# Moving rounding steps and masks, a fourth buffer for keys and values, and a last chunk in token order, in a kernel of retention and a feed-forward block

## Chip, cores, metric

One core of a Trainium2 chip. Time is device microseconds (us) of one execution; all runs quoted are of the fast state, except half_pe, of which there is one run whose state is unknown. GB/s is what the core's 16 DMA engines moved; a DMA share of 1.0 means that their packets took, summed, as long as 16 engines have. PE is TensorE, DVE VectorE, ACT ScalarE, POOL GpSimd, SP SyncE; SPq and ACTq are the DMA-issuing queues. "In the chain" means in the profile's chain of work that ended last, which gives a start and a length without overlap.

## The reference

```python
q, k, v: (8, 8, 576, 64)                 # batch, heads, tokens, width
scores = q @ k.T / 8
ret = scores * gamma_h ** (i - j) for i >= j, else 0
attn = ret @ v
x = attn.transpose(0, 2, 1, 3).reshape(4608, 512)
h = x @ w_in                             # 512 x 2048
g = h * erf(softplus(h))
out = g @ w_out                          # 2048 x 512; w_in and w_out arrive as float64
```

## The kernel before

Tokens are handled in 36 pieces of 128 and 9 chunks of 4 pieces; a piece is attended with a running state, so it needs queries and keys transposed, and keys and values in rows. From piece 8 on the transposed ones are loaded as squares (`load_squares`) that DVE transposes. The feed-forward block is cut in four quarters of `w_in` and `w_out`; the first quarter (`g == 0`) of each chunk runs interleaved with attention, the rest (from about 350 us on) alone. Both products use a seven-product scheme for 2 x 2 blocks. The weights arrive as 64-bit words and are rounded to float32 in steps, spread over the blocks. In the profile's lines qT and kT are transposed queries and keys, s on PE the scores, sT the masked scores, o on PE the outputs of attention; a, e and g are the PSUM accumulators of the feed-forward products, wraw the words, wa and wb the rounded weights. All products of two tensors on DVE go through one helper, L99.

```python
def load(i, names="qkv"):                                   # all issued by SP, in program order
    ...
        elif name == "q":
            t["qs"] = load_squares(i, "q", q)               # 4 DMAs each, 2 buffers, rows of 896 bytes
            t["ks"] = load_squares(i, "k", k)
        elif name == "v" or len(pieces[i]) == 1:
            t[name] = load_rows(i, name, src, 3)            # 2 DMAs, 3 buffers, rows of 256 bytes

def transposes(i): ...;  load(i + 2, "q")                   # DVE, then the next squares
def scores(i): ...                                          # PE s, then the masks sT on DVE (L99)
def outputs(i): ...;     load(i + 3, "kv")                  # PE o, then x scaled on DVE

def rounding():                                             # a generator: each next() is one step
    while True:
        ...
        nc.scalar.activation(a_f, high_f, AF.Abs)           # L246: ACT waits here for the words
        yield
        nc.vector.tensor_scalar(...)                        # L251, then L255, L259, L264
        ...
        load_weights()                                      # next words, on SP
        if sums: yield from sums(...)

# the block that loads words, n = 1 and 2:
            if n in (1, 2):
                load_weights()
                load_weights()
            run(b.middle(), (1, 1))                         # one rounding step after each product
            firsts[n - 1].sums()
            run(seconds[n - 1].first(), (1, 1))
            run(b.last())
```

Of the kernel before, what the change touches and what calls it, by code (L numbers as in the profile page):

```python
# [15 lines left out]
ALU = mybir.AluOpType  # L16
PSUM = bass.MemoryType.PSUM

P = 128
B, H, S, D = 8, 8, 576, 64  # L20
D_MODEL, D_FF = 512, 2048
NP = H // 2
# [32 lines left out]
def kernel(  # L55
# [15 lines left out]
    n_ch = n_tok // TCH  # L71
# [26 lines left out]
    def tt(out, in0, in1, op):  # L98
        nc.vector.tensor_tensor(out=out, in0=in0, in1=in1, op=op)  # L99

    def flat(ap):
        return ap.rearrange("p h d -> p (h d)")
# [17 lines left out]
    SQ = 32  # L120
# [14 lines left out]
    def load_rows(i, name, src, bufs):  # L135
        if name == "q":
            t = raw.tile([P, NP, P * D // SQ], FP32, tag="qs", name="raw_q", bufs=bufs)
            t = t.rearrange("p a x -> p (a x)")[:, : H * D].rearrange("p (h d) -> p h d", h=H)
        else:
            t = raw.tile([P, H, D], FP32, tag=name, name=f"raw_{name}", bufs=bufs)  # L140
        for b, s0, n, r0 in pieces[i]:
            for e in range(2):
                heads = src[b, e * NP : (e + 1) * NP, s0 : s0 + n, :]
                nc.sync.dma_start(out=t[r0 : r0 + n, e::2, :], in_=heads.rearrange("h p d -> p h d"))
        return t

    def load(i, names="qkv"):
        if i < len(pieces):
            t = loaded.setdefault(i, {})
            for name in names:  # L150
                src = {"q": q, "k": k, "v": v}[name]
                if name == "q" and i < SQUARES:
                    t["q"] = load_rows(i, "q", q, 2)
                elif name == "q":
                    t["qs"] = load_squares(i, "q", q)
                    t["ks"] = load_squares(i, "k", k)
                elif name == "v" or len(pieces[i]) == 1:
                    t[name] = load_rows(i, name, src, 3)

    load(0)  # L160
    cst = cpool.tile([P, CONST_COLS], FP32, name="cst")
# [4 lines left out]
    gk, gq, gp, tri, gk2, gq2, tri2 = (cst[:, a:b] for a, b in zip(ends, ends[1:]))  # L166
    gq, gq2 = (g.rearrange("p (a i) -> p a i", a=NP) for g in (gq, gq2))
# [108 lines left out]
    def round_weights(n=1):  # L276
        for _ in range(n):
            next(round_step, None)
# [7 lines left out]
    x = {}  # L286
# [55 lines left out]
    def outputs(i):  # L342
        segments = pieces[i]
        t = live.pop(i)
        seen = [(kept[b], r0, n) for b, s0, n, r0 in segments if s0 > 0]



        b, s0, n, _ = segments[0]
        o = [ps_at.tile([P, NP, P], FP32, tag="at", name=f"o{j}") for j in range(2)]  # L350
        for p in range(NP):
            for e in range(2):
                nc.tensor.matmul(  # L353
                    o[p % 2][heads[(e + p) % 2], p // 2, :],
                    lhsT=t["v"][:, 2 * p + e, :],
                    rhs=t["sT"][:, e, p, :],
                    start=(p < 2),
                    stop=(not seen and p >= NP - 2),
                    skip_group_check=True,
                )  # L360
        for state, r0, m in seen:
            for p in range(NP):
                for e in range(2):
                    nc.tensor.matmul(  # L364
                        o[p % 2][heads[(e + p) % 2], p // 2, r0 : r0 + m],
                        lhsT=state[heads[e], p, :],
                        rhs=t["qT"][heads[e], p, r0 : r0 + m],
                        start=False,
                        stop=(p >= NP - 2),
                        skip_group_check=True,  # L370
                    )
        if n == P:
            kv = flat(o[0])[:, 2 * P :].rearrange("p (a d) -> p a d", a=NP)
            for p in range(NP):
                for e in range(2):
                    nc.tensor.matmul(  # L376
                        kv[heads[e], p, :],
                        lhsT=t["k"][:, 2 * p + e, :],
                        rhs=t["v"][:, 2 * p + e, :],
                        start=False,  # L380
                        stop=(p == NP - 1),
                        skip_group_check=True,
                    )
        c, at = i // PC, i % PC * P
        if (0, c) not in x:
            x[0, c] = x_tile()

        def scaled(j):
            by = (gq if n == P else gq2)[:, j::2, :].unsqueeze(2).to_broadcast([P, 2, P // n, n])
            dst, got = (  # L390
                y.rearrange("p a (m i) -> p a m i", i=n) for y in (x[0, c][:, j:NP:2, at : at + P], o[j][:, :2])
            )
            tt(dst, got, by, ALU.mult)

        scaled(1)
        if n == P:
            sums = kv
            if s0 > 0:
                sums = att.tile([P, NP, D], FP32, tag="sums", name="sums")
                tt(sums, kv, kept[b], ALU.add)  # L400

            if b % 2 == 0 and s0 + P + D == S:
                new = att.tile([P, NP, D], FP32, tag="last", name="last", bufs=1)
            else:
                new = att.tile([P, NP, D], FP32, tag="state", name="state")
            (nc.gpsimd if s0 > 0 else nc.vector).tensor_tensor(out=new, in0=sums, in1=gp, op=ALU.mult)
            kept[b] = new
        scaled(0)
        load(i + 3, "kv")
        if i + 1 >= SQUARES:  # L410
            weigh_values(i + 1)
# [148 lines left out]
    class Second:  # L560
# [91 lines left out]
        def store(self, half, os=slice(0, D_MODEL), queue=nc.sync, tps=(0, 1)):  # L652
            if self.g < n_g - 1:
                nc.sync.dma_start(out=od[self.c][:, half, :, os], in_=self.o[:, half, :, os])
            else:
                for tp in tps:
                    for b, s0, n, r0 in pieces[self.c * PC + 2 * half + tp]:
                        rows = out[b * S + s0 : b * S + s0 + n, os].rearrange("(r a) o -> a r o", r=SQ)
                        for a in range(n // SQ):
                            at = slice(r0 + a * SQ, r0 + (a + 1) * SQ)  # L660
                            queue.dma_start(out=rows[a], in_=self.o[at, half, tp, os])
# [3 lines left out]
    firsts = [First(g, c) for g, c in order]  # L665
    seconds = [Second(f) for f in firsts]
# [15 lines left out]
    def run(steps, rounds=(), stages=1):  # L682

        for step, _ in enumerate(steps):
            attend(min(done[0] + stages, most[0]))
            round_weights(rounds[step] if step < len(rounds) else 0)
# [25 lines left out]
    most[0] = before_chunk(3)  # L712
    attend(after_chunk(1) + 1)
    operands_x(0, 1)
    round_weights(4)
    for _ in firsts[1].first():
        attend(done[0] + 1)
        round_weights(2)
    firsts[0].erf()
    firsts[0].multiply()  # L720
    seconds[0].begin()
    for b, nxt in zip(blocks[1:], blocks[2:] + [None]):
        n = order.index((b.g, b.c))
        if isinstance(b, First):
            most_g[0] = order[n - 1][0] + 1
            if n in (1, 2):
                load_weights()
                load_weights()
            run(b.middle(), (1, 1))
            firsts[n - 1].sums()  # L730
            run(seconds[n - 1].first(), (1, 1))
            run(b.last())
            most[0] = before_chunk(n + 3)
        elif n + 2 < n_s:
            f = firsts[n + 1]
            for step, _ in enumerate(b.middle()):
                attend(min(done[0] + 1, most[0]))
                if step == 0:
                    f.erf()
                elif step == 1 and n + 2 >= n_ch:  # L740
                    operands_x(*order[n + 2])
            if n + 2 < n_ch:
                attend(after_chunk(n + 2))
                operands_x(*order[n + 2])
            run(nxt.first(), (1,))
            f.multiply()
            seconds[n + 1].begin()
            if n_ch <= n + 3 < n_s:
                load_x(*order[n + 3])
            run(b.last(), (0, 1))  # L750
        elif n + 1 < n_s:
            firsts[n + 1].erf()
            seconds[n + 1].begin()
            rest = b.rest()
            for _ in range(3):
                next(rest)
            firsts[n + 1].multiply()
            run(rest)
            firsts[n + 1].sums((0,))
            first = nxt.first()  # L760
            next(first)
            firsts[n + 1].sums((1,))
            run(first)
        else:
            run(b.rest())
# [30 lines left out]
```

## Time and profile before

| | before |
|---|---|
| median of 3 runs | 1044.54 us (1043.72 to 1046.25) |
| profiled span, granted clock | 1041.5 us, 0.994 |
| PE busy | 1019.4 us, 98% |
| longest wait of PE | 5.8 us, at 87 to 93 us |
| end of span after the last sum | 6.7 us |

The prediction below shows the lines and how they are read. Another view is engines' busy time by stretch (us:us, length, then busy us and instructions of PE, PEld, DVE, ACT, POOL, then granted clock, DMA share, GB/s). Before:

```profile
60.00:100.00 40.00, 31.24 (x255) 24.55 (x255) 32.12 (x54) 13.36 (x17) 12.06 (x11) 0.87 0.98 226
100.00:150.00 50.00, 50.00 (x501) 40.63 (x498) 37.89 (x63) 18.27 (x23) 14.34 (x15) 1.00 0.85 207
150.00:200.00 50.00, 50.00 (x494) 40.49 (x494) 38.95 (x68) 14.81 (x21) 9.52 (x10) 1.00 1.02 223
```

### The profile page before, as it was taken

What the parts mean: (1) busy time and instruction counts of PE and PEld (TensorE: products, weight loads), DVE (VectorE), ACT (ScalarE), POOL (GpSimd) and SP (SyncE); (2) the same over time, 40 slices, a digit from 0 to 9 for tenths busy, and PEclk for the clock granted to TensorE, in tenths of its full rate; (3) what the DMA queues carried; (4) which work ended last, traced back from release to release, by engine and by line L of the source; (5) the groups of instructions that cost most, each with busy time, mean ns of one, the idle gap of its engine ahead of it and who ended that gap; (6) DMA issues with size and microseconds to landing.
All of it is one profiled execution on the core that took longest, in us unless ns stands there. A gap on an engine that the chain in (4) does not pass through costs nothing.

```text
span 1041.5 us, 15938 instructions
## 1 busy us (share of the span) xinstructions
PE 1019.4 (98%) x6322; PEld 875.6 (84%) x6322; DVE 674.9 (65%) x1061; ACT 387.6 (37%) x477; POOL 123.6 (12%) x122
## 2 busy tenths in 40 slices
PE   8987999999999999999999999999999999999997
PEld 7776888888888888888888888888888888888886
DVE  3996878768866645667656656666667555555554
ACT  2352242332342444433434334444443333333431
POOL 2160222221312000100001001100100000000000
PEclk9998999999999999999999999999999999999999
DMA  9989979999994531633264523363333334444433
GB/s 193 215 218 216 237 166 247 222 204 231 215 210 139 188 123 40 243 142 143 69 253 145 179 81 142 146 237 123 121 122 121 124 129 132 130 132 124 145 96 82
DMA packets 149051, 167.28 MB, mean 161 GB/s; under 512 B 97904, under 2 KB 123632, under 8 KB 140912
## 3 DMA queue, kind: packets, MB, share of 16 engines
q1 hardware_dynamic: 147824, 165.47, 55.9%
q8 instruction: 50, 0.82, 0.4%
q10 hardware_dynamic: 1152, 0.79, 0.3%
q14 instruction: 25, 0.20, 0.1%
HBM read 119.02 MB, written 47.19 MB: 160 GB/s over the span
## 4 chain that ended last, share of the span: by engine, by line
PE 87%; DVE 5%; DMA 5%; SPq 1%; issue 1%; ACT 1%; DVEq 0%; ACTq 0%
PE a L576 23%; PE a L469 22%; PE g L576 12%; PE g L469 11%; PE e L576 6%; PE e L469 6%; PE s L335 3%; PE o L353 2%; DMA wraw<-in_moe_w_in_dram 1%; PE o L376 1%; PE o L364 1%; DMA raw_qs<-in_q_dram 1%; DVE x L99 1%; DMA raw_ks<-in_k_dram 1%; DVE t L99 1%
## 5 line engine op out<-in xcount | busy, mean ns | idle before, releaser
L469 PE MATMUL a<-x,wa 128*128 128x256 f32 x1120 | 267.3, 382 | 0.0
L469 PEld LDWEIGHTS a<-x,wa 128*128 128x128 f32 x1120 | 212.4, 191 | 29.9 <-issue 0.2
L576 PE MATMUL a<-wb,s 128*128 128x256 f32 x864 | 205.7, 381 | 0.0
L576 PEld LDWEIGHTS a<-wb,s 128*128 128x128 f32 x864 | 162.9, 190 | 23.6 <-ACT o L590 0.7
L99 DVE TENSOR_TENSOR t<-g,t 128x512 f32<-128x512 f32 x70 | 48.3, 690 | 156.0 <-ACT t L499 116.0
L469 PE MATMUL g<-x,wa 128*128 128x256 f32 x560 | 133.8, 382 | 0.2 <-DVE o L99 0.2
L469 PEld LDWEIGHTS g<-x,wa 128*128 128x128 f32 x560 | 106.1, 191 | 15.6 <-DVE o L99 0.6
L99 DVE TENSOR_TENSOR o<-a,o 128x512 f32<-128x512 f32 x108 | 74.2, 687 | 50.5 <-PE a L576 50.5
L494 ACT COPY t<-a 128x512 f32<-128x512 f32 x35 | 20.5, 586 | 187.5 <-PE a L469 187.5
L99 DVE TENSOR_TENSOR t<-t,s 128x1024 f32<-128x1024 f32 x72 | 87.4, 1254 | 0.0
L538 ACT ACTIVATE s<-t 128x1024 f32<-128x1024 f32 x72 | 72.1, 1049 | 31.2 <-DVE t L99 31.2
L266 POOL TENSOR_TENSOR wraw<-wraw 128x512 f32<-128x512 f32 x28 | 29.1, 1040 | 455.2 <-DVE wraw L264 243.4
L99 DVE TENSOR_TENSOR x<-x 128x512 f32<-128x512 f32 x116 | 77.9, 704 | 1.2
L505 ACT COPY t<-a 128x512 f32<-128x512 f32 x35 | 20.5, 586 | 152.6 <-PE a L469 152.6
L542 ACT ACTIVATE s<-s 128x1024 f32<-128x1024 f32 x72 | 72.1, 1049 | 0.4
L576 PE MATMUL g<-wb,s 128*128 128x256 f32 x288 | 68.6, 381 | 0.1
L576 PE MATMUL e<-wb,t 128*128 128x256 f32 x288 | 68.6, 381 | 0.0
L576 PE MATMUL a<-wb,t 128*128 128x256 f32 x288 | 68.5, 380 | 0.0
L576 PE MATMUL g<-wb,t 128*128 128x256 f32 x288 | 68.2, 380 | 0.0
L99 DVE TENSOR_TENSOR o<-g,o 128x512 f32<-128x512 f32 x72 | 49.3, 685 | 27.5 <-ACT o L590 22.7
L469 PE MATMUL e<-x,wa 128*128 128x256 f32 x280 | 66.8, 381 | 0.0
L99 DVE TENSOR_TENSOR sT<-s,cst 128x512 f32<-128x512 f32 x72 | 46.2, 682 | 25.9 <-PE s L335 25.9
(75 smaller groups left out, 1201.3 us busy)
## 6 DMA issues: line engine op xcount, KB each, us to landing
od<-o SPq DMA_DIRECT2D x54, 512.0 KB, 3.3
x<-xd SPq DMA_DIRECT2D x27, 1024.0 KB, 5.0
o<-od SPq DMA_DIRECT2D x27, 1024.0 KB, 4.8
raw_qs<-in_q_dram SPq DMA_DIRECT2D x96, 112.0 KB, 4.6
raw_ks<-in_k_dram SPq DMA_DIRECT2D x96, 112.0 KB, 4.3
xd<-x SPq DMA_DIRECT2D x9, 1024.0 KB, 5.1
raw_k<-in_k_dram SPq DMA_DIRECT2D x64, 128.0 KB, 4.4
raw_v<-in_v_dram SPq DMA_DIRECT2D x64, 128.0 KB, 4.4
```

What stands on the lines that cost most here:

```text
L99: nc.vector.tensor_tensor(out=out, in0=in0, in1=in1, op=op)
L266: engine.tensor_tensor(out=r_f, in0=high_f, in1=r_f, op=ALU.mult)
L335: nc.tensor.matmul(ps[e][:, p, :], lhsT=t["kT"][heads[e], p, :], rhs=t["qT"][heads[e], p, :], start=True, stop=True)
L353: nc.tensor.matmul(o[p % 2][heads[(e + p) % 2], p // 2, :], lhsT=t["v"][:, 2 * p + e, :], rhs=t["sT"][:, e, p, :], start=(p < 2), stop=(no ...
L364: nc.tensor.matmul(o[p % 2][heads[(e + p) % 2], p // 2, r0 : r0 + m], lhsT=state[heads[e], p, :], rhs=t["qT"][heads[e], p, r0 : r0 + m], s ...
L376: nc.tensor.matmul(kv[heads[e], p, :], lhsT=t["k"][:, 2 * p + e, :], rhs=t["v"][:, 2 * p + e, :], start=False, stop=(p == NP - 1), skip_gr ...
L469: nc.tensor.matmul(acc[:, j * TH : (j + 1) * TH], lhsT=weights["wa", self.g][:, a, d, j * P : (j + 1) * P], rhs=x[self.g, self.c][a][:, d, :],
L494: nc.scalar.copy(out=self.t1[:, 1], in_=self.a)
L505: nc.scalar.copy(out=self.t2[:, 0], in_=self.a)
L538: nc.scalar.activation(self.s[:, j], t, AF.Softplus)
L542: nc.scalar.activation(self.s[:, j], self.s[:, j], AF.Erf)
L576: nc.tensor.matmul(acc[:, tp, :], lhsT=left[:, j * TH + tp * P : j * TH + (tp + 1) * P], rhs=weights["wb", self.g][:, b, j, :], start=(sta ...
```

## The change

The intent: DVE and ACT shall not stand at rounding steps whose words are still on their way (steps taken out of the block n = 1, one more step later in each block of chunks 2 to 8); the masks that PE waits for come before rounding; loads of keys and values wait less for buffers; the last chunk's `x` is put in token order already when scaled, so that its result can be stored with few DMAs.

```diff
-                    t[name] = load_rows(i, name, src, 3)
+                    t[name] = load_rows(i, name, src, 4)
...
         def scaled(j):
+            to = x[0, c][:, j:NP:2, at : at + P]
+            if c < n_ch - 1:
...                (as before)
+            for r0 in range(0, P, n):
+                dst = to[:, :, r0 : r0 + n].rearrange("p h (r a) -> p h a r", r=SQ)
...                (got and by as "p h (a r) -> p h a r")
+                tt(dst, got, by, ALU.mult)
...
+                        if self.c == n_ch - 1:
+                            queue.dma_start(out=out[b * S + s0 : b * S + s0 + n, os], in_=self.o[r0 : r0 + n, half, tp, os])
+                            continue
...
-    round_weights(4)
-    for _ in firsts[1].first():
+    for step, _ in enumerate(firsts[1].first()):
         attend(done[0] + 1)
-        round_weights(2)
+        round_weights((4, 2)[step])
...
-            run(seconds[n - 1].first(), (1, 1))
-            run(b.last())
+            run(seconds[n - 1].first(), (1, 1) if n > 1 else ())
+            run(b.last(), (1,) if 1 < n < n_ch else ())
```

More of the change, by code (lines that the diff above doesn't have):

```diff
@@ L388, in scaled @@
         def scaled(j):
-            by = (gq if n == P else gq2)[:, j::2, :].unsqueeze(2).to_broadcast([P, 2, P // n, n])
-            dst, got = (
-                y.rearrange("p a (m i) -> p a m i", i=n) for y in (x[0, c][:, j:NP:2, at : at + P], o[j][:, :2])
-            )
-            tt(dst, got, by, ALU.mult)
+            to = x[0, c][:, j:NP:2, at : at + P]
+            if c < n_ch - 1:
+                by = (gq if n == P else gq2)[:, j::2, :].unsqueeze(2).to_broadcast([P, 2, P // n, n])
+                dst, got = (y.rearrange("p a (m i) -> p a m i", i=n) for y in (to, o[j][:, :2]))
+                tt(dst, got, by, ALU.mult)
+                return
+            for r0 in range(0, P, n):
+                dst = to[:, :, r0 : r0 + n].rearrange("p h (r a) -> p h a r", r=SQ)
+                got, by = (
+                    y.rearrange("p h (a r) -> p h a r", r=SQ)
+                    for y in (o[j][:, :2, r0 : r0 + n], (gq if n == P else gq2)[:, j::2, :])
+                )
+                tt(dst, got, by, ALU.mult)
         scaled(1)
@@ L658, in store @@
                         rows = out[b * S + s0 : b * S + s0 + n, os].rearrange("(r a) o -> a r o", r=SQ)
+                        if self.c == n_ch - 1:
+                            queue.dma_start(
+                                out=out[b * S + s0 : b * S + s0 + n, os], in_=self.o[r0 : r0 + n, half, tp, os]
+                            )
+                            continue
                         for a in range(n // SQ):
```

## The prediction

> **What bounds the kernel now.** I read the page first, then the waits of TensorE, then the chain of work in order of time, then the timeline of the stretches where that chain leaves TensorE.
>
> The page says that TensorE (PE) is the bound, with a soft start:
>
> ```profile
> PE 1019.4 (98%) x6322; PEld 875.6 (84%) x6322; DVE 674.9 (65%) x1061; ACT 387.6 (37%) x477; POOL 123.6 (12%) x122
> ...
> PE   8987999999999999999999999999999999999997
> ...
> PEclk9998999999999999999999999999999999999999
> ...
> DMA  9989979999994531633264523363333334444433
> ```
>
> One digit is 26 us. From the fifth digit to the last but one PE is full; the change removes no matmul, so nothing can be won there. Only the first four digits (to about 103 us) and the last one are open. The chain in order of time agrees: from 350 to 1034 us it is one unbroken run of "PE a", "PE g", "PE e" pieces of 8 matmuls in 1.73 us. The waits of PE then give the size of the largest hole:
>
> ```profile
> PE s L335 <- DVE kT L314: 6.8, 3, 5.8
> ```
>
> Three waits, 6.8 us, the longest 5.8. The timeline shows where and why (start, length, engine, line; in brackets the idle time before it and its releaser):
>
> ```profile
> 82.34 2.49 SPq L229 DMA_DIRECT2D wraw<-in_moe_w_in_dram  x4
> ...
> 85.27 1.99 PE L576 MATMUL e<-wb,t 128*128 128x256 f32 x8
> ...
> 88.88 0.66 ACT L246 ACTIVATE wa<-wraw 128x512 f32<-128x512 f32 x1 [17.34 <-DMA wraw<-in_moe_w_in_dram]
> ...
> 89.57 0.43 DVE L251 TENSOR_SCALAR wa<-wa 128x512 f32<-128x512 f32 x1 [5.84 <-ACT wa L246]
> ...
> 91.20 0.70 DVE L314 STREAM_TRANSPOSE qT<-raw_qs 128x512 f32<-128x512 f32 x1
> 91.83 1.04 DVE L314 STREAM_TRANSPOSE kT<-raw_ks 128x512 f32<-128x512 f32 x1
> ...
> 93.02 2.08 PE L335 MATMUL s<-qT,kT 64*128 64x128 f32 x16 [5.76 <-DVE kT L314]
> 95.03 3.11 PE L469 MATMUL a<-x,wa 128*128 128x256 f32 x8
> ```
>
> The words of the next weights are issued at 82.34 and land at 88.88. ScalarE and VectorE already stand at the rounding of these words: ACT was idle for 17.34 us before it, DVE for 5.84. Behind that rounding step in DVE's queue stand the transposes that PE needs, although their data was issued by 76.6 us. So PE stands still for 5.76 us, and starts again slowly: the 16 score matmuls take 2.08 us (1.09 at 104.03 in the chain), the next 8 span 3.04 us of the chain (1.92 elsewhere).
>
> A smaller hole lies just before it: rounding of wb occupies DVE from 69.74 to 71.8 us, and the masks come after it:
>
> ```profile
> 71.72 1.28 DVE L99 TENSOR_TENSOR sT<-s,cst 128x512 f32<-128x512 f32 x2
> ...
> 72.50 2.19 PE L353 MATMUL o<-sT,raw_v 128*64 128x128 f32 x16 [1.58 <-issue]
> ```
>
> At the end, the stores of the last chunk queue up on the sync queue (SPq) behind each other:
>
> ```profile
> 1018.49 18.18 ACTq L661 DMA_DIRECT2D out_dram<-o  x19
> ...
> 1022.13 16.84 SPq L661 DMA_DIRECT2D out_dram<-o  x24
> ...
> 1034.08 0.69 DVE L99 TENSOR_TENSOR o<-a,o 128x512 f32<-128x512 f32 x1 [1.04 <-PE a L576]
> ```
>
> The last sum ends at 1034.77, but SP issues until 1038.97 and the span ends at 1041.5.
>
> **What the Trainium skill says.** "TensorE: Matmul & The Clock Gate", section "Architectural detail": ACT and DVE are strict FIFO. The trace agrees: no transpose passes the rounding step that waits for words. The same page, "What's actually happening": after an idle window of about 3.4 us TensorE falls to half clock until a window was busy again. It agrees roughly: after 5.76 us of idle the granted clock is 0.66 in 90 to 100 us, and the scores take 1.9 times as long. "DMA: Bandwidth & Descriptors", section "Anatomy of one DMA": a DMA's semaphore wait is done by the issuing sequencer, so a load that waits for a buffer holds up the loads behind it; and about 2 us are fixed per transfer. Here stores land 1.7 us after issue (median). "SBUF — State Buffer", section "Door 1": lines of 16 bytes, each new line costs. A write with a step of four floats touches a new line every time; here the transpose that writes so (kT) takes 927 ns, the one that writes in order (qT) 632.
>
> **The change, part by part.**
>
> *Rounding out of the block that loads words.* The order of instructions of the changed kernel shows that the first rounding of the new words moves from row 100 to row 144 on DVE, some five pieces of attention later; on ACT it stands 11 places later. PE's order and the first 60 groups of SP's order stay the same. The transposes at 91.20 then wait only for ACT's copy of a product that PE finished at about 81.5, and for data long landed. DVE was done with its masks at 83.7; one weight sum (0.6), the sum t (0.7), qT (0.6) and kT (1.0) bring it to about 86.6, before PE's 87.26. Gain 5.76. With no idle there is no slow restart: 2.08 - 1.09 = 0.99 and 3.04 - 1.92 = 1.12, together 2.1. **Gain 7.9 us.** The rounding steps are made up by one more step per block for chunks 2 to 8, where PE is the bound and DVE has 10 to 20% left.
>
> *Masks ahead of rounding.* The masks start at 69.8 instead of 71.72, so the 16 matmuls of L353 start when PE is free (70.92): 1.58 of idle and 2.19 - 1.09 = 1.1 of stretching go, and 0.56 of slow clock on the following 8 matmuls and 0.40 before the next scores, 3.6 at most. But two of the four weight sums now come later: 0.6 in front of the next masks, and the sums wait for GpSimd about 0.4 longer there. From kT to those masks DVE needs 4.6 + 0.6 for the first + 0.4 = 5.6 us, PE from the scores to its need of them 1.09 + 1.83 + 1.82 = 4.7. So about 1.0 to 1.4 come back. **Gain 2.2 us.**
>
> *Four buffers.* No instruction changes; a load of keys and values waits for a buffer freed one piece earlier. To 103 us the sync queue waited at those loads (L144) 5.7 us in all, for example about 1.4 at 14 us ahead of the first words. That would start the rounding chain of the start earlier; but DMA shares there are 0.91 and 1.03, so most of it is a transfer limit. PE's own losses at 20 to 36 us are about 3.5. I take **1.0 us**.
>
> *Last chunk in token order.* Stores of 32 rows become stores of whole pieces: of the last chunk 12 issues on SP become 4 and 12 on ACT become 3. SP's 16 stores of the chunk before took 7.36 us, 0.46 each. Now: 8 issues from 1033.05 plus 4 make the 1038.97 seen. After: 3 issues end at 1034.4, one after the last sum ends at 1035.3, and so does ACT's one. That is 3.7 earlier; larger transfers may land some 0.7 later. **Gain 3.0 us.** The price: eight scalings of 256 elements (0.413 us each) now write with the step of four. By kT's ratio 927/632 that is 0.19 each, about 1.5 us of DVE around 280 to 330 us, beside a full PE. Nothing on the path.
>
> Sum: 7.9 + 2.2 + 1.0 + 3.0 = 14.1.
>
> **The rivals.** *DMA takes the stall's place.* From 60 to 100 us the DMA share is 0.88, 1.09, 1.07, 0.88 at 183 to 273 GB/s; taking 10 us out asks for the same bytes in 30 us, which is more than any window shows. For it: the 100 to 320 us that follow are also near 1.0, and DVE waited for raw_ks ten times (9.0 us in all). Against: PE waits for none of this after 103 us, loads run about one piece ahead, stores of x and o can slip. At worst it takes back 6 us: 1036 to 1037. *DVE becomes the bound of the attention stage.* It is 9.97 of 10 us busy in 270 to 280 and 310 to 320, and gets the displaced rounding and the stepped writes (about 5 us in 230). Against: PE reads 10.00 there, so DVE has some lead. It would cost 1 to 3 us: 1033 to 1035. *The start is bound by SP after all*, and four buffers shift the whole rounding chain from 23 us on by 2 to 3 us: 1029 to 1030. *The words are waited for again, later*: they land by 89, the step now stands near 100, so I give it little.
>
> For the first two rivals together I take 1.5 us off: 14.1 - 1.5 = 12.6. From the median of 1044.5: **1032 us**, or a span near 1029.
>
> **Range and chances.** With the second rival of the start instead of mine, and nothing given back, 1044.5 - 16.5 = 1028. With half of the mask and start gains lost and the DMA taking some 5 us, 1037. So 1028 to 1037. Faster by over 2% means below 1023.7, 21 us less: more than all idle time that I could find, so 0.04. Slower by 2% would need a new stall of 33 us: 0.01. Within 2%: 0.95.
>
> **What would show it.** Right: the wait of s L335 for kT L314 falls from 6.8 to below 1.5 us; ACT's 17.34 us of idle for words is gone; granted clock 0.95 or more from 80 to 100 us; the pieces that stood at 103 us stand at about 92; issues end within 1.5 us of the last sum, and the span 3 to 4 us after it. Masks: L353 after x stands at 1.1 us, with a small new wait in the next outputs. Wrong: idle PE between 90 and 330 us for raw_ks, raw_v or sT (first two rivals); the gap at 85 to 93 merely renamed to a DMA; a start to 60 us that moves by over 2 us; or a tail of stores that stays at 6 us because landing, not issue, holds it.

## The result

The changed kernel took 1040.01 us (median of 4 runs, 1036.58 to 1040.78) against 1045.15 of before: ratio 0.9945, 95% interval 0.9919 to 0.9972. (Ratios here are the mean time of one kernel's runs over that of the other's of the same rounds, so not quite the ratio of the medians.) A later measurement (after_again below) gave 0.9933. The forecast was 1032, in a range of 1028 to 1037: about half of the gain is missing.

The stall itself is gone. The timeline of the changed kernel, with the same products as in the prediction (lines of the file moved by 9 from the scaling on):

```profile
84.92 2.00 PE L585 MATMUL e<-wb,t 128*128 128x256 f32 x8
86.84 1.16 PE L335 MATMUL s<-qT,kT 64*128 64x128 f32 x16
87.94 2.00 PE L478 MATMUL a<-x,wa 128*128 128x256 f32 x8
```

No idle time stands in brackets, and the clock is full. The next scores, at 104.03 us before, are at 95.82: PE is 8.2 us ahead. But at about 320 us the product "a", which follows the same outputs, began at 320.19 before and begins at 320.60 now: all 8.2 us and 0.4 more were lost in between. The lines, the scores from the chain and the product from the timeline, before:

```profile
104.03 1.09 PE s L335 x16
...
320.19 1.99 PE L469 MATMUL a<-x,wa 128*128 128x256 f32 x8
```

and in the changed kernel:

```profile
95.82 1.09 PE s L335 x16
...
320.60 1.99 PE L478 MATMUL a<-x,wa 128*128 128x256 f32 x8
```

The timeline of the changed kernel shows where; here the lines of PE, of SP's issues and of DVE's transposes are put in one order of time:

```profile
140.59 1.16 PE L335 MATMUL s<-qT,kT 64*128 64x128 f32 x16 [1.00 <-DVE kT L314]
...
158.69 1.16 PE L335 MATMUL s<-qT,kT 64*128 64x128 f32 x16 [0.32 <-DVE kT L314]
...
175.06 0.89 SPq L229 DMA_DIRECT2D wraw<-in_moe_w_out_dram  x1
176.04 1.96 SPq L130 DMA_DIRECT2D raw_qs<-in_q_dram  x4
176.18 1.16 PE L335 MATMUL s<-qT,kT 64*128 64x128 f32 x16 [0.37 <-DVE kT L314]
178.10 4.18 SPq L130 DMA_DIRECT2D raw_ks<-in_k_dram  x4
...
184.11 0.71 DVE L314 STREAM_TRANSPOSE qT<-raw_qs 128x512 f32<-128x512 f32 x1 [4.12 <-DMA raw_qs<-in_q_dram]
188.08 1.08 DVE L314 STREAM_TRANSPOSE kT<-raw_ks 128x512 f32<-128x512 f32 x1 [3.26 <-DMA raw_ks<-in_k_dram]
189.31 2.08 PE L335 MATMUL s<-qT,kT 64*128 64x128 f32 x16 [4.16 <-DVE kT L314]
191.32 3.78 PE L478 MATMUL a<-x,wa 128*128 128x256 f32 x8
```

DVE now stands idle at its transposes because the queries and keys have not landed, 4.12 and 3.26 us, and PE behind it. It stands so before the scores at 140.59 (2.61 and 1.69 us) and at 176.18 (2.13 and 0.59 us) too; only the 0.32 us at 158.69 stand behind DVE's own sums. Four idle times make 1.00 + 0.32 + 0.37 + 4.16 = 5.85 us. After the long one TensorE starts at the low clock again: 2.08 - 1.09 = 0.99 for the scores and, in the chain, 3.71 - 1.92 = 1.79 for the product. The sum is 8.6 us, just what was lost. The wait has kept its name in the list of PE's waits (6.8 us, 3 times before), but its cause is another:

```profile
PE s L335 <- DVE kT L314: 7.2, 6, 4.2
```

The stretches say what lies under it:

```profile
60.00:100.00 40.00, 36.12 (x339) 28.70 (x338) 36.29 (x59) 18.31 (x21) 14.04 (x13) 1.00 0.98 220
100.00:150.00 50.00, 49.00 (x491) 39.51 (x491) 36.41 (x63) 14.64 (x20) 10.49 (x11) 1.00 0.96 215
150.00:200.00 50.00, 45.09 (x416) 36.49 (x415) 36.77 (x65) 12.30 (x16) 12.33 (x13) 0.93 1.01 224
```

The GB/s are those of before within 4% in each row. PE came 8 us early, the data did not.

The start and the masks gave less than foreseen. The first product of chunk 1 begins at 63.70 us (63.43 before). The masks let the outputs start without a gap, but two new ones follow:

```profile
71.12 1.29 PE L353 MATMUL o<-sT,raw_v 128*64 128x128 f32 x16
...
79.84 1.99 PE L585 MATMUL a<-wb,t 128*128 128x256 f32 x8 [1.14 <-DVE t L99]
82.89 0.40 PE L353 MATMUL o<-sT,raw_v 128*64 128x128 f32 x2 [1.05 <-issue]
```

The tail did what it should. The last sum ends at 1035.46 and the span at 1038.9, so 3.4 us after it (6.7 before):

```profile
1027.15 8.71 ACTq L669 DMA_DIRECT2D out_dram<-o  x3
...
1033.76 2.21 SPq L669 DMA_DIRECT2D out_dram<-o  x4
1034.77 0.69 DVE L99 TENSOR_TENSOR o<-a,o 128x512 f32<-128x512 f32 x1 [1.03 <-PE a L585]
```

### The profile page after: what moved, and what is told of

It reads as the page before. It is cut to its first block, busy times and chain, and to the rows that moved or that the text cites. A ratio compares the mean times of both kernels' runs of the same rounds, so it can differ in the third digit from the quotient of the medians.

```text
span 1038.9 us, 15904 instructions
## 1 busy us (share of the span) xinstructions
PE 1018.9 (98%) x6322; PEld 876.6 (84%) x6322; DVE 675.8 (65%) x1063; ACT 388.1 (37%) x477; POOL 125.3 (12%) x122
## 2 busy tenths in 40 slices
DMA packets 148778, 167.27 MB, mean 161 GB/s; under 512 B 97632, under 2 KB 123360, under 8 KB 140640
## 4 chain that ended last, share of the span: by engine, by line
PE 84%; DMA 6%; DVE 4%; SPq 4%; ACT 1%; issue 1%; POOL 0%; DVEq 0%; POOLq 0%; ACTq 0%
PE a L585 22%; PE a L478 22%; PE g L585 11%; PE g L478 11%; PE e L585 6%; PE e L478 5%; PE s L335 2%; PE o L353 2%; SPq L144 2%; DMA raw_qs<-in_q_dram 1%; SPq L130 1%; DMA wraw<-in_moe_w_in_dram 1%; DMA wraw<-in_moe_w_out_dram 1%; DMA raw_ks<-in_k_dram 1%; PE o L376 1%; DMA raw_v<-in_v_dram 1%
```

## Experiments

Theory: the transfers of the attention stage set its pace as much as PE does; time won ahead of them is waited for again. Rivals: the fourth buffer lets keys and values push ahead of the next queries and keys; the words stand at a bad place in the one queue; or what counts in the transfers is the number of DMAs rather than the work in the DMA engines. All ratios below are to the kernel before in the same rounds.

| run | median us | ratio (95%) |
|---|---|---|
| rounding_only | 1041.24 | 0.9967 (0.9945 to 0.9990) |
| bufs_only | 1044.64 | 0.9998 (0.9977 to 1.0019) |
| last_only | 1041.78 | 0.9973 (0.9953 to 0.9994) |
| no_bufs | 1038.36 | 0.9943 (0.9924 to 0.9963) |
| after_again (the changed kernel) | 1039.69 | 0.9933 (0.9916 to 0.9951) |
| few_words (wrong result) | 1029.84 | 0.9855 (0.9835 to 0.9874) |
| kv_on_act | 1074.13 | 1.0280 (1.0257 to 1.0303) |
| words_on_pool | 1036.70 | 0.9919 (0.9903 to 0.9935) |
| half_pe (wrong result, one run) | 899.3 | |
| split_kv | 1094.9 | 1.0456 (1.0435 to 1.0477) |
| merged_kv | 1038.06 | 0.9917 (0.9900 to 0.9935) |
| merged_words | 1036.01 | 0.9896 (0.9880 to 0.9911) |
| wide_kv (wrong result) | 1031.54 | 0.9867 (0.9850 to 0.9883) |

### The parts alone

rounding_only: the two last hunks of the diff alone.

> The kernel before with only the rounding steps and the masks moved. Theory (transfers set the pace of the attention stage, so time saved at 85 to 93 us is waited again before 200 us): the 5.76 us stall is gone and the scores after it stand 7 to 9 us earlier, but PE then waits 4 us or more for raw_qs and raw_ks between 120 and 200 us, and the whole is only 0 to 4 us faster than before. Rival (the fourth buffer for keys and values lets their loads ahead and starves q and k): without the buffer no such wait comes, and the whole is 8 to 10 us faster.

bufs_only: `load_rows(i, name, src, 4)` alone.

> The kernel before with four buffers for keys and values and nothing else. Transfer theory: within 1 us of before, the 5.76 us stall stays. My prediction's part: 1 us faster. Rival (the buffer starves q and k): 1 to 4 us slower.

last_only: the scaling and the stores of the last chunk alone.

> The kernel before with only the last chunk in token order. All theories: the end of the span after the last sum falls from 6.7 to about 3.4 us, 3 to 3.5 us faster in all; DVE's slower scaling near 290 to 330 us costs nothing on PE.

no_bufs: the changed kernel with `load_rows(i, name, src, 3)`.

> The changed kernel with three buffers again. Transfer theory: within 1.5 us of the changed kernel, so 3 to 7 us faster than before, with the same kind of wait for raw_ks before 200 us. Rival (the buffer starves q and k): 11 to 13 us faster than before.

Measured: rounding_only is 3.0 us below the median of before (1044.26), its first scores after the stall stand at 94.88 (104.03 before), and PE then waits four times, 5.4 us in all and 2.8 at most, for kT between 100 and 334 us, where the kernel before has no wait. In its profiled run, one of its slowest, the product near 320 us begins at 319.95, 0.24 us ahead of before: nearly all of the 9 us is waited for again, without any fourth buffer. bufs_only shows no gain (its interval of about 2 us either way could hide 1 us), and no_bufs is as fast as the changed kernel, with 4.6 us of the same waits: the buffer rival falls. last_only is 2.5 us below the median of before (0.9973 of it is 2.8); its span ends 3.5 us after the last sum. The parts add up.

### Fewer bytes, other queues, less work for PE

few_words:

```diff
-                nc.sync.dma_start(out=t[rows].rearrange("p (h f) -> p h f", h=2), in_=src)
+                m = WP if part[2] == 0 else WP // 8
+                view = t[rows].rearrange("p (h f) -> p h f", h=2)
+                if m < WP:
+                    nc.gpsimd.memset(view[:, :, m:], 0)
+                nc.sync.dma_start(out=view[:, :, :m], in_=src[:, :, :m])
```

> The changed kernel, but of the weight words of the second to fourth quarter only an eighth of the bytes is loaded, by as many DMAs (the rest is zeroed by GpSimd; a wrong result on purpose). Theory (the attention stage waits because the bytes in the DMA engines set its pace): PE's waits for kT between 100 and 200 us fall from 6 to under 2 us, and the whole is 4 to 8 us faster than the changed kernel, 10 to 13 faster than before. Rival (the number of issues on the one sync queue sets the pace): the waits stay, within 2 us of the changed kernel.

The waits for kT fall to 1.3 us in the whole run, none is left between 100 and 330 us, and the time to 1029.84. Stretch and wait of few_words:

```profile
150.00:200.00 50.00, 50.00 (x491) 40.74 (x490) 40.53 (x66) 14.66 (x20) 15.98 (x15) 1.00 1.04 234
```

```profile
PE s L339 <- DVE kT L318: 1.3, 2, 0.7
```

With the transfers lightened nothing is given back: the second scores stand at 94.42 us (103.96 before in the same view), 9.5 us ahead, and the first product after attention begins at 339.79 (349.81), 10.0 us ahead. With 3.3 us of the tail this makes the 13.3 us between the two profiled spans (1041.5 and 1028.2).

kv_on_act:

```diff
-                nc.sync.dma_start(out=t[r0 : r0 + n, e::2, :], in_=heads.rearrange("h p d -> p h d"))
+                queue = nc.scalar if i > SQUARES and name in "kv" else nc.sync
+                queue.dma_start(out=t[r0 : r0 + n, e::2, :], in_=heads.rearrange("h p d -> p h d"))
```

> The changed kernel, with the loads of keys and values from piece 9 on issued by ScalarE's queue: same bytes, a third fewer issues per piece on the sync queue. Bytes theory: within 2 us of the changed kernel. Issue theory: PE's waits for kT between 100 and 200 us fall under 2 us, 4 to 8 us faster than the changed kernel.

29 us slower than before, which neither theory expected. The run does not tell them apart, because it added a wait: in the order of instructions every DMA of SP and ACT takes one of eight completion semaphores in turn and waits for the DMA that had it last. SP stood 70.0 us at its square loads behind keys that ACT had issued late, and ACT's own work queued behind its issues.

words_on_pool:

```diff
-                nc.sync.dma_start(out=t[rows].rearrange("p (h f) -> p h f", h=2), in_=src)
+                queue = nc.sync if part[2] == 0 else nc.gpsimd
+                queue.dma_start(out=t[rows].rearrange("p (h f) -> p h f", h=2), in_=src)
```

> The changed kernel, with the weight words of the second to fourth quarter issued by GpSimd's queue, so that they no longer stand in the sync queue ahead of queries and keys: same bytes. Theory of place (what hurts is only that 0.5 to 1 MB of words stand ahead of the next queries and keys in one queue): the wait of 4 us at 185 us goes and it is 3 to 8 us faster than the changed kernel. Bytes theory: within 2 us.

Correct and 8.3 us below the median of before; against the changed kernel the gain is 1.5 to 3 us (its ratio 0.9919 against 0.9933 and 0.9945). The waits for kT fall to 2.4 us, none above 0.7. In its profiled run, its fastest, PE is 7.86 us ahead at the second scores and 5.64 at the last, so 2.2 us were given back, where the two profiled runs of the changed kernel gave back 8.6 and 5.3 (the second also its fastest). So moving the words has a share that may be about half. It takes their place ahead of queries and keys and their issues off SP's queue at once; this run does not separate the two.

half_pe: in both feed-forward products one of two accumulated matmuls is left out.

```diff
-                for d in range(2):
+                for d in range(1):
...
-            for j in range(GP):
+            for j in range(1):
```

> The changed kernel with half of the matmuls of both feed-forward products left out from the second chunk on (a wrong result on purpose), transfers and the other engines' work unchanged. Transfer theory: the attention stage hardly shrinks; its last load of values is still issued at 290 us or later (316 in the changed kernel), with PE waiting for kT for tens of us. Rival (PE sets the pace of the stage from 200 us on, as its unbroken chain says): it shrinks with PE's work, until VectorE is full, to 270 us or less.

The last values are issued from 308.4 to 311.4 us (313.3 to 316.2 in the changed kernel), although PE has half of its feed-forward work. The DMA rates stay at 210 to 238 GB/s. PE now waits in this stage too, for kT and for values among others (whole run):

```profile
PE s L335 <- DVE kT L314: 20.9, 13, 7.7
PE o L353 <- POOL raw_v L301: 18.7, 11, 3.2
```

So without half of PE's work the stage still needs about as long. The DMA rates, and DVE waiting 28.5 us for queries and keys between 100 and 330 us, say that the transfers hold it; but PE also waits 11.7 us there for sums of DVE, which is busy for 37 to 40 of 50 us. From this run alone the transfers as the only limit are argued, not shown.

### Number of DMAs, or work in the DMA engines

after_again is the changed kernel beside the next three.

> The changed kernel itself, beside the next three on one chip: 5 to 6 us faster than before, with 4 to 9 us of PE's waits for kT between 100 and 200 us.

Its profiled run spans 1035.9 us: 7.9 us ahead at the second scores (96.16), 2.6 ahead at the product near 320 us (317.56). Thus this run gave back 5.3 us and that of the result 8.6: how much is lost varies from run to run, which fits the spread of the changed kernel's times (1036.58 to 1041.82; those of few_words lie within 0.4 us). Of the 5.3 us, 1.17 are a wait of a product for DVE's sum t at 223.70; it stands behind transposes that had waited 1.43 and 1.85 us for queries and keys.

split_kv:

```diff
-                nc.sync.dma_start(out=t[r0 : r0 + n, e::2, :], in_=heads.rearrange("h p d -> p h d"))
+                cuts = 2 if i > SQUARES and name in "kv" else 1
+                for z in range(cuts):
+                    at = slice(z * n // cuts, (z + 1) * n // cuts)
+                    nc.sync.dma_start(out=t[r0 : r0 + n][at, e::2, :], in_=heads[:, at, :].rearrange("h p d -> p h d"))
```

> The changed kernel, each load of keys and values from piece 9 on cut into two of 64 rows: same bytes and same rows of 256 bytes, but 4 DMAs more per piece on the sync queue, on which every DMA waits for the one eight before it to land (the order of instructions names eight semaphores in turn). Theory that the bytes in the DMA engines set the pace: within 2 us of the changed kernel. Rival that the number of DMAs sets it (issue time of 0.46 us each, or at most eight in flight): 15 us or more slower, with PE waiting for kT or for values all through the attention stage.

merged_kv: keys and values of later pieces keep the heads' own order, so that one DMA of 256 KB brings them.

```diff
+            if i > SQUARES and name in "kv":
+                nc.sync.dma_start(out=t[r0 : r0 + n], in_=src[b, :, s0 : s0 + n, :].rearrange("h p d -> p h d"))
+                continue
...                (weights of values and the three products take the heads from their new places)
```

> The changed kernel, the two loads of keys (and of values) of a piece from piece 9 on made one of 256 KB, heads in their own order: same bytes, 10 DMAs per piece for 12. Bytes theory: within 2 us of the changed kernel. Number theory: PE's waits for kT between 100 and 200 us fall below 2 us, 4 to 8 us faster than the changed kernel, near 1032 us.

merged_words: both, merged_kv and words_on_pool.

> The merged loads together with the weight words on GpSimd's queue, a version that may beat both kernels. Bytes theory: like the words on GpSimd's queue alone, some 8 us faster than before. Number theory: 12 to 14 us faster than before, near 1031 us, no wait for kT over 1 us.

split_kv is 55 us slower than the changed kernel, which the pure bytes theory did not expect; merged_kv, with fewer DMAs, is only 1.6 us faster, its interval overlapping that of the changed kernel, which the pure number theory did not expect. The stretch of split_kv, then of merged_kv:

```profile
150.00:200.00 50.00, 39.28 (x344) 31.43 (x344) 28.09 (x49) 9.01 (x13) 7.87 (x8) 0.93 0.72 176
```

```profile
150.00:200.00 50.00, 49.03 (x488) 39.91 (x485) 41.03 (x68) 14.04 (x19) 15.15 (x19) 1.00 1.10 235
```

In split_kv the DMA engines are not full (0.72); SP issued 44 to 52 DMAs per 30 us, as in the changed kernel (43 to 49), and was occupied 28 to 29 of each 30 us: there the number of DMAs is the limit, about 0.6 us each with the gaps. In merged_kv 34 to 43 DMAs per 30 us moved about the same GB/s at a share of 1.0 to 1.1: there the engines are the limit. The changed kernel lies where both limits meet. It is the time of the issues and not the eight in flight: from 100 to 300 us SP's waits in split_kv sum to 14 us, 5.5 of them for DMAs to land (31 and 16 us in the changed kernel), and for nearly all the rest of these 200 us it issues. A half load of keys took 0.61 us to issue (median), a whole one 0.42 in the changed kernel, so the edit made issues longer as well as more; why is not shown. merged_words is the fastest correct version tried: 1036.01 us, ratio 0.9896 to before, below both kernels.

wide_kv:

```diff
+                if i > SQUARES and name in "kv":
+                    at = (s0 + e * S * NP) * D
+                    block = src[b].rearrange("h s d -> (h s d)")[at : at + n * NP * D]
+                    nc.sync.dma_start(out=t[r0 : r0 + n, e * NP : (e + 1) * NP, :], in_=block.rearrange("(p h d) -> p h d", h=NP, d=D))
+                    continue
```

> The changed kernel, each load of keys and values from piece 9 on taking rows of 1 KB instead of 256 bytes, from other tokens (a wrong result on purpose): same bytes, same number of DMAs, a quarter of the packets. Theory that bytes set the pace: within 2 us of the changed kernel, with 4 to 9 us of waits for kT. Rival that the number of small packets keeps the DMA engines busy: the waits fall below 2 us, the DMA share between 100 and 200 us falls below 0.9, and it is 6 to 10 us faster than the changed kernel, near 1030 us.

The time falls to 1031.54 us and the waits for kT to 1.3 us in the whole run, none between 100 and 330 us; packets fall from 148,778 to 109,610, bytes stay at 167.27 MB. Stretches of wide_kv:

```profile
100.00:150.00 50.00, 50.00 (x498) 40.42 (x498) 39.05 (x68) 15.34 (x21) 10.70 (x12) 1.00 0.83 218
150.00:200.00 50.00, 50.00 (x488) 40.94 (x487) 42.29 (x68) 14.73 (x20) 16.25 (x15) 1.00 0.99 265
```

The share does not stay below 0.9 in both stretches, as the packet rival had it, but the engines move 265 GB/s where they moved 224. So not the bytes as such set the pace but the time that bytes in rows of 256 take in the DMA engines. My theory of plain bytes falls; few_words had lightened the same engines by another way.

## Why the prediction was wrong

- **The bound.** "From the fifth digit to the last but one PE is full ... nothing can be won there." Nothing could be won, but something lost. In the attention stage PE was one of two resources that were full. A view read for the other was at hand: share 0.98, 0.85, 1.02 by stretch, and SP occupied 27.5 to 28.5 of each 30 us from 120 to 300 us. I looked at the first and not at the second. The Trainium skill names this sign: "Perfetto Trace Analysis", section "What 'DMA-bound' means", says that a kernel is bound by the issuing sequencer when its track is solid DMA slices, or by the engines, and that large descriptors help in both cases. split_kv shows the first, wide_kv the second.
- **The step that failed** is the term taken off for the rivals: "For the first two rivals together I take 1.5 us off". The first of them was the right mechanism ("DMA takes the stall's place"), even with the signs named (idle PE for raw_qs and raw_ks between 90 and 330 us). Its size was 8.6 us in one profiled run and 5.3 in another, not 1.5, and "at worst 6" was too little. What I set against it ("loads run about one piece ahead") was read in a run that lagged because of the stall: the stall gave the transfers their lead. bufs_only and last_only, which keep the stall, have no wait for kT between 100 and 334 us. The second rival, DVE, had 0.32 us of it at most: at the other three waits it stands idle at its transposes.
- **Rounding out of the loading block, 7.9 us:** right. 8.2 us ahead at the next scores, of which about 0.35 stood before the stall. The words are no longer waited for.
- **Masks, 2.2 us:** too much. With the start 0.27 us later, the product at 85 us begins 0.35 us earlier: 0.6. The 1.58 us gap and the stretching went (3.3 us up to the next scores), but the product "a" waits 1.14 us for t and the next outputs 1.05 us, and about 0.5 us are lost around these two gaps. I counted what the delayed weight sums cost the masks, not that they also stand before t, which a product of PE needs first.
- **Four buffers, 1.0 us:** not seen (bufs_only 0.9998, 0.9977 to 1.0019). SP's waits at these loads to 103 us fall from 5.7 to 3.3 us, but the loads of keys at 13 us take as long as before (2.49 and 2.37 us). That the transfers of the start are the limit there is not shown.
- **Tail, 3.0 us:** 3.3 in the trace (6.7 to 3.4), 2.8 by the ratio of last_only. The stepped scaling costs about 0.2 us more for each instruction of 256 elements, as worked out from the transposes, but there are six of these and not eight: the mean of 70 is 431 ns, and 64 of them at 413 leave 0.62 us for each of the six. PE waited for none.

In the sum: 7.9 + 0.6 - 0.3 + 3.3 = 11.5 came; 8.6 went back, and 0.3 at the end of attention (0.49 us of idle near 350 us for 0.22): 2.6 us, the difference of the two profiled spans. The median run keeps 5 to 7. Where the transfers are eased (few_words, wide_kv), 14 to 15 us are kept by the ratios, 13.3 and 11.0 by the profiled spans.

## What to carry to other kernels

A stage in which PE has no wait may still run at the pace of its transfers: look whether the DMA share is near 1.0 and the issuing queue occupied without a gap before you book time won ahead of it. This is a warning and no proof: few_words and wide_kv show shares of 0.83 to 1.04 from 100 to 200 us, and PE waits for nothing there. Test it by cutting bytes, cutting rows or adding DMAs, each alone; they are different limits. Here time won at the end of the kernel, behind all loads, was kept (2.8 us in last_only), and time won at the front was mostly taken back by the next full resource.

## What the Trainium skill lacked or had wrong

- "DMA: Bandwidth & Descriptors", section "Bandwidth", gives its measured rates for plain loads, and says that small descriptors are slow, but gives no rate for many loads of 256-byte and 896-byte rows mixed with stores. Here the engines are full at 215 to 235 GB/s with them, and reach 265 when the rows of keys and values are 1 KB (wide_kv).
- No page has what a program that gives its DMAs eight completion semaphores in turn runs into: 29 us lost when two queues share the semaphores (kv_on_act). No page has the time to issue one DMA from SP as measured on this chip ("DMA: Bandwidth & Descriptors" has a count of cycles for earlier generations, in a part about trn3): here 0.42 us for a load of keys and 0.61 for half of it (medians), and a queue full of issues at a DMA share of 0.72 to 0.76 (split_kv, 100 to 300 us).
- "SBUF — State Buffer", section "Door 1", has the 16-byte lines without a duration: here writing with a step of 16 bytes makes a DVE product of 256 elements about 0.62 us instead of 0.41.
- "TensorE: Matmul & The Clock Gate", section "What's actually happening", puts half clock after an idle window of about 3.4 us. The runs agree after longer idle times (after 4.16 us products lost 2.8 us more, after 5.76 us 2.1), but show it after shorter ones too: after 2.56 us of idle in no_bufs the granted clock is 0.50 from 187.3 to 190.7 us and the scores take 2.08 us, and after 1.58 us in the kernel before it is 0.50 from 73.5 to 76.8 us. After 1.98 us at 32 us in the changed kernel it stays full. So a wait below 3.4 us can cost a slow restart as well; which ones do is not shown.
